# A two-layer FNet and gated-MLP kernel: layer 2's down products of blocks two to four in seven products for eight

## The chip, the cores and the metric

The kernel runs on one core of one Trainium2 chip. The time is the device time of one execution, in microseconds, and what counts is the median of several runs. TensorE (PE) multiplies matrices out of SBUF into PSUM banks; VectorE (DVE), ScalarE (ACT) and GpSimd (POOL) work on tiles; SyncE (SP) issues most of the DMA transfers. Each engine works through its own instructions in the order in which they stand.

## The reference, cut to what matters

```python
def layer(x):                      # x: 2048 x 640, fp32; run twice
    n = layernorm(x)
    a, b = n @ hid_re.T, n @ hid_im.T            # DFT along the hidden axis
    x = x + seq_re @ a - seq_im @ b              # DFT along the sequence, real part
    n = layernorm(x)
    h = sigmoid(n @ w_gate) * (n @ w_up)         # 640 -> 1728
    return x + h @ w_down                        # 1728 -> 640
```

The DFT matrices are inputs. The three weights are random with a spread of 0.4 (0.05 times 8). All is fp32.

## The kernel before, in words

**Numbers in two parts.** TensorE works on f16. Each operand is the sum of a high part (a cast, on ScalarE) and a low part (what the cast left, on VectorE), and each product takes three passes, high by high, high by low and low by high (`PASSES`). `split` (L266) makes the parts of a weight.

**Tokens and tiles.** The 2048 rows of x lie in SBUF as 16 tiles of 128, in four blocks of four (here called blocks 1 to 4; the code counts from 0). A block's four tiles are called GA, GB, GC and GD; for the DFT they hold even and odd rows of two halves of the sequence. The 1728 columns of the gated part are 13 tiles of 128 and half a tile.

**One layer.** First the DFT, folded by the symmetries of its matrices. Then each block in turn goes through gate and up, and then down. A step of gate and up does two of the 13 tiles, j and j+1, for the block's 512 tokens, and the half tile comes last. From layer 2's block 1 and layer 1's block 2 on, gate and up already run as seven products of 256 columns where the plain way has eight (`seven`; `part_one` to `part_seven` are its products, L1446, and what empties PSUM): sums of the quarters of x and of the weights are multiplied, and sums of the results are the four quarters wanted. What the previous pair of tiles still needs (the gate's sigmoid, the multiplication by up in `up`, and the cast and low part in `up_parts`, L1508 to L1514) is worked off within the next pair's step. `gate_tail` (L1585 to L1590) does the half tile.

**Down** is plain in both layers: for each of the block's four row tiles and each half of the 640 columns, 13 x 3 + 2 products of 320 columns (L1603), added into x by one VectorE instruction a half (L1618). A row tile of layer 2 is then stored by `store_x` (L438): GA and GD by SP's queue (L447), GB and GC by rows, from POOL's queue (L442), the very last from ACT's.

**The next block's x.** While a block is worked on, x of the next one is normalised and turned, in pairs of row tiles: `pair_apply` and `pair_combine` (L603 to L614) and `pair_parts` (L621, L622) on VectorE and ScalarE, then two transposing transfers on SP's queue (`pair_transpose`, L628). They are written into one of two buffers `XW`; `place` (L574) says which, by turns.

**Weights.** Their f16 parts and the sums for the seven products are made in layer 1 and kept in DRAM; `load_s` (L1362) brings a tile's parts back on SP's queue for each block. `test_w` (L262 in its cost: a largest absolute value) tests in layer 2 that the weights lie within bounds.

**Tests of symmetry.** The folding is right only if the DFT matrices have the symmetries, so the matrices are read beside the work, in pieces: a load on POOL's queue (L1664, L1681, L1724), a few operations of VectorE (`test_rows`, L1670 to L1673, and the like), and squares summed up on ScalarE (L1636). At the end a flag is read, and where it is set a general path computes all anew. Before, 51 of the 84 tests of the sequence's matrices are in layer 1, and the tests of the hidden ones are in layer 2, block 3 and later.

**What sets the order.** The program is a list of steps (14 slots of gate and up and 8 of down a block). A table of calls `at(u, f)` puts each job at a place u in units of steps, and the jobs of a step are written out ahead of its products, or at four places within a `seven` step. SBUF is one tile `big`, whose pieces get their addresses from a planner (`find_homes`) in a first pass.

```python
for j0, j1 in ((0, 7), (7, NF + 1)):
    steps.append(down(b, i, j0, j1, not first))
...
u = block[b] - 8 + 1.2 * i
...
at(u + 1.1, pair_transpose, b, i, not first and b == last)
```

## Time and profile before

| | us |
|---|---|
| median of three runs (lowest, highest) | 1135.03 (1135.00, 1135.28) |
| span of the profiled execution, first to last instruction | 1133.3 |
| TensorE busy | 1117.1 (99%) |
| VectorE busy | 757.7 (67%) |
| ScalarE busy | 539.9 (48%) |
| GpSimd busy | 346.8 (31%) |
| DMA, mean over the span | 189 GB/s |

The profiled execution's own time isn't among the three; its span leaves out what lies ahead of the first instruction and behind the last, 1.7 us against the median.

In the profile, "busy" counts an engine's working instructions. A row of a group reads: line of the code, engine, operation, destination <- source, count, busy time and mean time of one, and then the idle time ahead of them with what ended most of it. A row of waits reads: engine and what it stood for, what released it, and then the total, the count and the longest. A row of the chain of waits or of the timeline begins with the start in us and the duration. A window's row gives start and end, length, and then the busy time of PE, PEld, DVE, ACT, POOL with counts, the granted clock of TensorE, the busy share of the DMA engines and GB/s. Layer 2's blocks lie at these times of the trace: block 1 at 654 to 754 us, block 2's gate and up until 834 and its down until 878.5, block 3 until 958.4 and 1003, block 4 until 1083 and 1127.6.

### The profile page before, as it was taken

The page shows a single profiled execution, that of the slowest core. Times are in us where ns is not written, and L with a number is a line of the kernel's source. Part 1 is how long each engine was busy: PE and PEld are TensorE (multiplying, and loading weights), DVE is VectorE, ACT ScalarE, POOL GpSimd, SP SyncE. Part 2 cuts the span into 40 slices and gives each one's busy share as a digit, 9 for nine tenths or more (in the row PEclk, how much of TensorE's full clock was granted, in tenths as well). Part 3 has the DMA queues.
Part 4 walks back from the last instruction along what each step waited for, and adds up shares of the span by engine and source line. Part 5 has one row for each costly group of instructions (what it writes and reads, how often), then busy time and mean ns, then how long its engine had stood idle before and what let it go on. Part 6 is the DMA issues. An engine that isn't in the chain of part 4 may idle for free. (4 is left out here: it accounts for less than half of the span.)

```text
span 1133.3 us, 23690 instructions
## 1 busy us (share of the span) xinstructions
PE 1117.1 (99%) x9112; PEld 891.3 (79%) x9112; DVE 757.7 (67%) x1679; ACT 539.9 (48%) x1191; POOL 346.8 (31%) x568
## 2 busy tenths in 40 slices
PE   7999999999999999999999999999999999999997
PEld 5767446788878887788878888778877888788875
DVE  7984897856756776576667877834764678526751
ACT  7985583355525653256525545314542555225430
POOL 1001653343455354322340203031554222132001
PEclk9999999999999999999999999999999999999999
DMA  7633885878597756778521772585857873998411
GB/s 241 194 107 103 311 314 154 247 221 256 156 223 225 256 183 159 205 240 309 165 94 53 195 228 83 136 234 179 257 172 171 280 256 103 115 247 261 167 42 39
DMA packets 154448, 214.74 MB, mean 189 GB/s; under 512 B 74655, under 2 KB 99505, under 8 KB 154326
## 3 DMA queue, kind: packets, MB, share of 16 engines
q1 hardware_dynamic: 135622, 165.04, 50.0%
q0 software_dynamic: 18560, 47.93, 14.4%
q8 instruction: 73, 1.20, 0.4%
...
## 5 line engine op out<-in xcount | busy, mean ns | idle before, releaser
L1446 PE MATMUL acc<-big 128*128 128x256 f16 x4698 | 516.4, 273 | 0.0
L1446 PEld LDWEIGHTS <-big 128*128 128x128 f16 x4698 | 459.7, 98 | 54.3
L1603 PE MATMUL acc<-big 128*128 128x320 f16 x2624 | 357.7, 299 | 0.0
L1603 PEld LDWEIGHTS <-big 128*128 128x128 f16 x2624 | 256.8, 98 | 99.5
L1450 ACT ACTIVATE big<-acc 128x256 f32<-128x256 f32 x348 | 131.1, 382 | 261.8 <-PE acc L1446 259.4
L1664 POOL DMA_DIRECT2D big<-in_ct x256 | 174.3, 686 | 249.5 <-DVE big L1673 110.3
L1514 DVE TENSOR_TENSOR big<-big 128x512 f16<-128x512 f32 x87 | 59.9, 688 | 111.6 <-ACT big L1513 111.5
L1636 ACT ACTIVATE big<-big 128x768 f32<-128x768 f32 (+10 forms) x110 | 81.3, 739 | 83.9 <-DVE big L1673 56.6
L1399 PE MATMUL acc<-big 128*128 128x256 f16 (+1 forms) x705 | 114.7, 325 | 0.3 <-ACT big L678 0.3
L1399 PEld LDWEIGHTS <-big 128*128 128x128 f16 x705 | 68.9, 98 | 44.9 <-issue 0.6
L1618 DVE SCALAR_TENSOR_TENSOR big<-acc,big 128x320 f32<-128x320 f32 x64 | 28.4, 483 | 74.3 <-PE acc L1603 74.3
L1492 ACT ACTIVATE big<-big 128x512 f32<-128x512 f32 x87 | 53.2, 627 | 44.5 <-DVE big L1483 43.8
L271 DVE SCALAR_TENSOR_TENSOR big<-big 128x640 f16<-128x640 f32 (+7 forms) x82 | 61.4, 779 | 11.1 <-ACT big L269 8.8
L1502 DVE SCALAR_TENSOR_TENSOR big<-acc,big 128x256 f32<-128x256 f32 x87 | 36.4, 418 | 48.2 <-PE acc L1446 42.7
L269 ACT ACTIVATE big<-big 128x640 f16<-128x640 f32 (+7 forms) x82 | 51.3, 658 | 21.0 <-POOL big L1337 6.6
L1483 DVE TENSOR_TENSOR big<-big,acc 128x512 f32<-128x512 f32 x87 | 59.2, 680 | 2.9 <-PE acc L1446 2.6
L1513 ACT ACTIVATE big<-big 128x512 f16<-128x512 f32 x87 | 54.4, 625 | 7.6 <-DVE big L1504 6.5
L1681 POOL DMA_DIRECT2D big<-in_ct x40 | 27.3, 688 | 92.2 <-ACT big L1636 55.9
L621 ACT ACTIVATE big<-big 128x384 f16<-128x384 f32 (+2 forms) x48 | 28.6, 646 | 52.3 <-DVE big L603 34.5
L442 POOL DMA_INDIRECT out<-big,rows x8 | 9.5, 1187 | 133.4 <-DVE fin L1761 53.6
L1482 DVE TENSOR_TENSOR big<-big 128x256 f32<-128x256 f32 x87 | 36.3, 417 | 8.8 <-ACT big L1450 8.7
L622 DVE TENSOR_TENSOR big<-big 128x384 f16<-128x384 f32 (+2 forms) x48 | 34.2, 750 | 7.1 <-DMA big<-big 7.0
(252 smaller groups left out, 1089.2 us busy)
## 6 DMA issues: line engine op xcount, KB each, us to landing
...
big<-kept_w SPq DMA_DIRECT2D x115, 320.0 KB, 4.8
big<-in_ct POOLq DMA_DIRECT2D x256, 128.0 KB, 5.1
...
kept_w<-big SPq DMA_DIRECT2D x27, 320.0 KB, 3.7
...
big<-in_wg SPq DMA_DIRECT2D x18, 320.0 KB, 4.9
```

Of the source, the lines that this page charges most:

```text
L269: nc.scalar.activation(dh, src, AF.Copy, scale=s)
L271: nc.vector.scalar_tensor_tensor(dl, src, s, dh, op0=OP.mult, op1=OP.subtract)
L1399: nc.tensor.matmul(ps, w[wp][:, d * P : (d + 1) * P], xt[:, xp, :], start=(d == 0 and wp == HI and xp == HI), stop=(d == ND - 1 and wp == LO))
L1446: nc.tensor.matmul(ps, wt, xt, start=start and n == 0, stop=n == len(todo) - 1, skip_group_check=not start)
L1450: nc.scalar.activation(dst, ps, AF.Copy)
L1483: nc.vector.tensor_tensor(v, v, other, op=OP.add)
L1492: nc.scalar.activation(v, v, AF.Sigmoid, scale=SG)
L1513: nc.scalar.activation(s.parts[HI], v, AF.Copy)
L1514: nc.vector.tensor_tensor(s.parts[LO], v, s.parts[HI], op=OP.subtract)
L1603: nc.tensor.matmul(held["pd", e][0][:, :EH], held["ht", j].parts[hp][:, i * P : (i + 1) * P], held["w", 2, j].parts[wp][:, e * EH : (e + 1 ...
L1636: nc.scalar.activation(v, v, AF.Square, accum_out=new_sum()[:p])
L1664: nc.gpsimd.dma_start(v[:, g], bass.AP(ct.tensor, (r * S + row) * S, [[P, NS], [d * S, 16], [1, P]]))
```

## The change

**Down in seven products.** In layer 2's blocks 2 to 4 (`MADE`), twelve of the F tiles are taken as six pairs (`mates`). The pair is the inner dimension's two halves, the rows of the left side are {GA, GB} and {GC, GD}, and the columns are the two halves of 320. `mated_down` multiplies seven combinations (A11, A12, A22 and sums S1 to S4 of the left, three halves of the weights and four combinations of them on the right), for two row tiles each, into PSUM banks that are added into x at several points: 16 adds a block where there were 8. The 13th tile and the half tile stay plain. `mates_sums` makes the four sums of a pair on VectorE, `mates_parts` and `mates_rest` the casts and low parts of seven quarters where there were four. The result of `part_seven` is now added straight from PSUM by VectorE, where ScalarE copied it out first (not in a block's last step).

**Weights.** The four combinations of each of the six pairs of down weights are made in layer 1's blocks 2 and 3 (`load_mates`, `make_mates`, `split_mates`, `keep_mates`), in the buffer of x that is free then, kept in DRAM, and loaded once in layer 2's block 2 (`load_t`) into places that have come free: one of the two buffers `XW` among them. From then on `place` gives blocks 2 to 4 of layer 2 the one that is left.

**Places.** The pair work on the next block's x stands later, and so do its transposes and the first weight loads. Each test of symmetry has its own places for load, work and squares in `TESTS` and `HIDDEN` (46 in layer 1, 38 in layer 2); `test_w` of the down weights moves from layer 2's block 3 into layer 1's downs (`DOWNS`). The stores of GB and GC of blocks 2 and 3 come after the next block's start (`block + 1.3`). Within the made downs, jobs are written out in between the products (`due`). The bound on the weights' size goes from 16 to 4.

```diff
-WMAX = 16.0
+WMAX = 4.0
...
+NP = 6
+MADE = {(1, 1), (1, 2), (1, 3)}
+TESTS = [(0, 1, 5.5, 6.7, 7.2), (0, 1, 12.5, 14.2, 14.7), (0, 1, 18.0, 19.2, 19.7), (0, 1, 18.5, 19.7, 20.2), (0, 1, 19.0, 20.2, 20.7), (0, 1, 20.0, 21.2, 21.7),
...
+DOWNS = [(0, 18.6), (0, 19.1), (0, 19.6), (0, 20.1), (1, 19.1), (1, 19.6),
...
+MATES = [(5.7, 7.2, 7.5), (7.3, 8.7, 9.0), (8.8, 11.2, 11.5), (5.7, 7.2, 7.5), (7.3, 8.7, 9.0), (8.8, 11.2, 11.5)]
...
     def place(b):
-        return (b + len(other)) % 2
+        return 0 if other and b else (b + len(other)) % 2
...
+    def load_mates(m):
+        for j in (2 * m, 2 * m + 1):
+            nc.sync.dma_start(fixed(made_at(m) + 5 * (j % 2), 5, "tr", j).f32, wd[j * P : (j + 1) * P, :])
+
+    def make_mates(m):
+        a, b = (held["tr", j].f32 for j in (2 * m, 2 * m + 1))
+        v = fixed(made_at(m) + 10, 10, "tf", m).f32
+        t1, t2, t3, t4 = (v[:, EH * n : EH * (n + 1)] for n in range(4))
+        nc.vector.tensor_tensor(t1, a[:, EH:], a[:, :EH], op=OP.subtract)
+        nc.vector.tensor_tensor(t3, b[:, EH:], a[:, EH:], op=OP.subtract)
+        nc.vector.tensor_tensor(t2, b[:, EH:], t1, op=OP.subtract)
+        nc.vector.tensor_tensor(t4, b[:, :EH], t2, op=OP.subtract)
+        for j in (2 * m, 2 * m + 1):
+            drop("tr", j)
+
...
+    def load_t(m):
+        pin = (0, 10, XU + XTU, XU + XTU + 10, XU + XTU + 20, FIX)[m]
+        nc.sync.dma_start(take(10, "T", m, pin=pin).f16, kept["t", m])
+
...
-    def part_seven(b, j):
+    def part_seven(b, j, last):
         chain, _, _, _, _, w = held["step", j]
         products(chain, b, j, [("S3", "T3"), ("UM", "x1M")])
-        snap(w[:, :256], chain)
-
-    def part_three(b, j):
+        if last:
+            snap(w[:, :256], chain)
+        else:
+            nc.vector.tensor_tensor(w[:, :256], chain, w[:, 256:], op=OP.add)
+
+    def part_three(b, j, last):
         _, _, other, ko, v, w = held["step", j]
         products(other[:, 256:], b, j, [("S4", "x11"), ("GM", "x1M")])
-        nc.vector.tensor_tensor(w[:, :256], w[:, :256], w[:, 256:], op=OP.add)
-        nc.vector.tensor_tensor(v, v, other, op=OP.add)
+        if last:
+            nc.vector.tensor_tensor(w[:, :256], w[:, :256], w[:, 256:], op=OP.add)
+        both = other.rearrange("p (h c) -> p h c", h=2)
+        nc.vector.tensor_tensor(v[1], v[1], both, op=OP.add)
...
+        if ("hv", j) not in held:
+            if j % 2:
+                mates_parts(j - 1, "hA")
+                mates.append(j - 1)
...

...
             up(earlier[0])
+            mates_sums()
             some(1)
             part_four(b, earlier[1])
             for i in js:
                 part_five(b, i)
             up_parts(earlier[0])
             up(earlier[1])
+            if not last:
+                mates_rest()
             some(2)
             if last:
                 tail(ps, 1)
                 drop("w", 3, 0)
             for i in js:
-                part_seven(b, i)
+                part_seven(b, i, last)
+            if last:
+                mates_rest()
...
+    A11, A12, A22, S1, S2, S3, S4 = range(7)
+
+    def mated_down(b, store):
+
+        accs = {}
+        last = b == NB - 1
+
+        def left(m, q, hp, p):
+            name, o = (("hA", 0), ("hA", 1), ("hB", 0), ("hS", 0), ("hS", 1), ("hR", 0), ("hR", 1))[q]
+            return held[name, 2 * m].parts[hp][:, 256 * o + P * p : 256 * o + P * (p + 1)]
+
+        def right(m, w, wp):
+            if w < 3:
+                return held["w", 2, 2 * m + (w > 0)].parts[wp][:, EH * (w == 2) : EH * (w == 2) + EH]
+            return held["T", m].parts[wp][:, EH * (w - 3) : EH * (w - 2)]
+
+        def products_of(p, n, q, w, start, stop):
+            out = [(m, hp, wp) for m in range(NP) for hp, wps in PASSES for wp in wps]
+
+            def one(k, m, hp, wp):
+                if (p, n) not in accs:
+                    accs[p, n] = bank()
+                nc.tensor.matmul(accs[p, n][0][:, :EH], left(m, q, hp, p), right(m, w, wp), start=start and k == 0,
+                                 stop=stop and k == len(out) - 1, skip_group_check=True)
+
+            return [(one, k, *t) for k, t in enumerate(out)]
+
...
+        def add(p, n, g, e, free):
+            ps, k = accs[p, n]
+            xe = X[:, b * TB + g, e * EH : (e + 1) * EH]
+            nc.vector.scalar_tensor_tensor(xe, ps[:, :EH], CB, xe, op0=OP.mult, op1=OP.add)
+            if free:
+                del accs[p, n]
+                free_bank(k)
+
...
+        todo = []
+        for p in range(2):
+            todo += products_of(p, "a", A11, 0, True, True) + [(add, p, "a", p, 0, False)]
+        for p in range(2):
+            todo += products_of(p, "c", A12, 1, True, False)
+        todo += [(done, "hA")]
+        for p in range(2):
+            todo += products_of(p, "a", S2, 4, False, True) + [(add, p, "a", p, 1, False)]
+        for p in range(2):
+            todo += plain(p, "c", p, 0, False) + [(add, p, "c", p, 0, True)]
+        for p in range(2):
+            todo += products_of(p, "d", S1, 3, True, True) + [(add, p, "d", p + 2, 1, False)]
+        todo += [(done, "hS")]
+        for p in range(2):
+            todo += products_of(p, "a", S3, 5, False, True) + [(add, p, "a", p + 2, 1, False)]
+        for p in range(2):
+            todo += plain(p, "e", p + 2, 1, True) + [(add, p, "e", p + 2, 1, True)]
+        for p in range(2):
+            todo += products_of(p, "a", A22, 6, False, False) + plain(p, "a", p + 2, 0, False)
+            todo += [(add, p, "a", p + 2, 0, True)] + ([(put, p + 2)] if last or p else [])
+            todo += [(done, "hB")] if p else []
+            q = 1 - p
+            todo += products_of(q, "d", S4, 2, False, False) + plain(q, "d", q, 1, False)
+            todo += [(add, q, "d", q, 1, True)] + ([(put, q)] if last or p else [])
+        marks = [n for n, t in enumerate(todo) if t[0].__name__ == "one"]
+        cuts = [0] + [marks[len(marks) * k // 8] for k in range(1, 8)] + [len(todo)]
+
+        def step(k):
+
+            def mm(due):
+                for n in range(cuts[k], cuts[k + 1]):
+                    if n == 38:
+                        mates_rest()
+                    if (n - cuts[k]) % 6 == 0 and n > 38:
+                        due((n - cuts[k]) / (cuts[k + 1] - cuts[k]))
+                    f, *a = todo[n]
+                    f(*a)
+                due(1)
+
...
+            return mm, post, False
+
+        return [step(k) for k in range(8)]
 
...
-            for i in range(TB):
+            for i in range(TB) if (layer, b) not in MADE else ():
...
+            if (layer, b) in MADE:
+                steps += mated_down(b, not first)
...
-                u = block[b] - 8 + 1.2 * i
+                slow = (layer, b - 1) in MADE
+                u = block[b] - 6.9 + 1.8 * i if slow else block[b] - 8 + 1.2 * i
...
-                    at(u + 0.2 + 0.2 * n, pair_parts, b, i, n)
-                at(u + 1.1, pair_transpose, b, i, not first and b == last)
+                    at(u + (0.4 + 0.3 * n if slow else 0.2 + 0.2 * n), pair_parts, b, i, n)
+                at(u + (1.5 if slow else 1.1), pair_transpose, b, i, not first and b == last)
...
-                        at(u - 2 - 0.5 * (j % 2) if j > 3 else block[b] - ((5.9, 3, 2, 1.5) if first and b == 1 else (8, 7.9, 4.5, 3.5))[j], load_s, j, not first and b == last)
+                        at(u - 2 - 0.5 * (j % 2) if j > 3 else block[b] - ((5.9, 3, 2, 1.5) if first and b == 1 else (4.5, 4, 3, 2.2) if (layer, b - 1) in MADE else (8, 7.9, 4.5, 3.5))[j], load_s, j, not first and b == last)
...
-                at(block[2] + j - 0.3, test_w, 2, j)
+                at(block[DOWNS[j][0]] + DOWNS[j][1], test_w, 2, j)
...
+        for m in range(NP):
+            if first:
+                u, v, w = (block[1 + m // 3] + t for t in MATES[m])
+                at(u, load_mates, m)
+                at(v, make_mates, m)
+                at(w, split_mates, m, (0,))
+                at(w + 0.5, split_mates, m, (1,))
+                at(w + 1.0, keep_mates, m)
+            else:
+                at(block[1] + 1 + m, load_t, m)
...
+                for g in (GB, GC) if made else ():
+                    at(block[b + 1] + 1.3, store_x, b, g, slice(0, D))
...
+        for (load, test, key), (l, b, u, v, w) in zip(tests, TESTS):
+            if l == layer:
+                at(block[b] + u, load, *key)
+                at(block[b] + v, test, *key)
+                at(block[b] + w, square_rest)
...
+        def due(part):
+            while todo and todo[0][0] - u <= part:
+                _, f, a = todo.pop(0)
+                f(*a)
```

How this moves instructions is shown at two places. The first is VectorE at the entry into layer 2's block 2's down, where the gate and up's last work stands in front of the adds. Before:

```order
L1587 SCALAR_TENSOR_TENSOR big<-acc_65,big 64x512
L1590 TENSOR_TENSOR big<-big 64x512
L1670 TENSOR_TENSOR big<-big 128x256
L1671 TENSOR_TENSOR big<-big 128x256
L1673 TENSOR_TENSOR big<-big 128x128 x2
L1482 TENSOR_TENSOR big<-big 128x256
L1483 TENSOR_TENSOR big<-big,acc_483 128x512
L1502 SCALAR_TENSOR_TENSOR big<-acc_64,big 128x256
L1504 SCALAR_TENSOR_TENSOR big<-big 128x256
L1514 TENSOR_TENSOR big<-big 128x512
```

After, the same stretch and what follows it (L1726 and L1729 are the half tile, L1577 and L1579 are `part_three`, L1628 to L1631 the four sums, L1599 and L1601 `up`, L1616 `up_parts`, L1807 the adds into x, L1640 the low parts of a pair):

```order
L1726 SCALAR_TENSOR_TENSOR big<-acc_65,big 64x512
L1729 TENSOR_TENSOR big<-big 64x512
L1577 TENSOR_TENSOR big<-big 128x256
L1579 TENSOR_TENSOR big<-big,acc_483 128x512
L1628 TENSOR_TENSOR big<-big 128x256
L1629 TENSOR_TENSOR big<-big 128x256
L1630 TENSOR_TENSOR big<-big 128x256
L1631 TENSOR_TENSOR big<-big 128x256
L1599 SCALAR_TENSOR_TENSOR big<-acc_64,big 128x256
L1601 SCALAR_TENSOR_TENSOR big<-big 128x256
L1616 TENSOR_TENSOR big<-big 128x512
L1807 SCALAR_TENSOR_TENSOR big<-acc_480,big 128x320
```

The test of rows (L1670 to L1673) has gone from here, four sums have come between `part_three` and `up`, and the first add into x stands right behind the last tile's low part.

The second is SP's queue ahead of layer 2's block 4, with the two transposing transfers of each pair of row tiles. Before:

```order
L1363 DMA big_63<-kept_w_0_0_1146 128x1280
L1365 DMA big_63<-kept_s_0_2103 128x2048
L1367 DMA big_63<-kept_w_1_0_1163 128x1280
L1363 DMA big_63<-kept_w_0_1_1182 128x1280
L1365 DMA big_63<-kept_s_1_2204 128x2048
L1367 DMA big_63<-kept_w_1_1_1199 128x1280
L628 DMA_TRANSPOSE big_63<-big_63 128x17x128 x2
L447 DMA out_0<-big_63 128x640
L628 DMA_TRANSPOSE big_63<-big_63 128x17x128 x2
L1363 DMA big_63<-kept_w_0_2_1253 128x1280
```

After (L679 are the transposes, L1447 to L1451 the loads of a tile's gate parts, sums and up parts):

```order
L679 DMA_TRANSPOSE big_63<-big_63 128x17x128 x2
L1447 DMA big_63<-kept_w_0_0_1146 128x1280
L1449 DMA big_63<-kept_s_0_2103 128x2048
L1451 DMA big_63<-kept_w_1_0_1163 128x1280
L1447 DMA big_63<-kept_w_0_1_1182 128x1280
L1449 DMA big_63<-kept_s_1_2205 128x2048
L1451 DMA big_63<-kept_w_1_1_1199 128x1280
L679 DMA_TRANSPOSE big_63<-big_63 128x17x128 x2
L1447 DMA big_63<-kept_w_0_2_1253 128x1280
```

The first pair's transposes now stand ahead of the loads of tiles 0 and 1, and the second pair's behind them; the store of a row tile between them is elsewhere.

233 lines of the change are left out of this document (160 added, 73 removed), and 13 rows, old and new, of the table TESTS.

## The prediction

> **What bounds the kernel now.** I read the page first, then what TensorE (PE) waited for, then the chain of waits.
>
> ```profile
> PE 1117.1 (99%) x9112; PEld 891.3 (79%) x9112; DVE 757.7 (67%) x1679; ACT 539.9 (48%) x1191; POOL 346.8 (31%) x568
> PEclk9999999999999999999999999999999999999999
> L1603 PE MATMUL acc<-big 128*128 128x320 f16 x2624 | 357.7, 299 | 0.0
> ```
> ```profile
> PE twin L404 <- DMA big<-in_x: 6.1, 3, 3.9
> ...
> PE acc L1036 <- DVE big L900: 0.8, 1, 0.8
> ```
> ```profile
> 709.51 44.55 PE acc L1603 x328
> ...
> 833.98 44.55 PE acc L1603 x328
> 878.53 71.40 PE acc L1446 x654
> ...
> 1083.02 44.57 PE acc L1603 x328
> ...
> 1127.62 0.49 DVE big L1618
> ```
>
> PE is busy 99% of the span at a granted clock of 0.9 or more in every slice. What it waits for lies at the start (twin, the turning of x) or between the layers (L1036, 0.8 us at most at once). From 709.5 us to the end the chain of waits is PE alone, one product behind the other. So in layer 2 each product removed shortens the program by its own spacing, as long as nothing else comes late. A down of one block is 328 products in 44.55 us, 0.1358 us each (the 299 ns of the group is one product's latency, not its spacing). A gate-and-up product of 256 columns takes 71.40 / 654 = 0.1092 us.
>
> **The change, part by part.**
>
> *Fewer products.* A block's down was 4 x 2 x (13 x 3 + 2) = 328 products. Now 12 of the 14 rows of tiles go in six pairs: 7 combinations x 2 x 6 pairs x 3 passes = 252, and the last two rows take 8 x (3 + 2) = 40. That is 292, so 36 fewer in each of three blocks: 108 x 0.1358 = **-14.67 us**, all on the path. The shape (128x320) stays.
>
> *VectorE (DVE) and ScalarE (ACT) in the gate-and-up steps.* For two rows of tiles, VectorE gets four sums of 256 columns, and the low parts are taken of 1,792 columns instead of 1,024.
>
> ```profile
> L1514 DVE TENSOR_TENSOR big<-big 128x512 f16<-128x512 f32 x87 | 59.9, 688 | 111.6 <-ACT big L1513 111.5
> L1482 DVE TENSOR_TENSOR big<-big 128x256 f32<-128x256 f32 x87 | 36.3, 417 | 8.8 <-ACT big L1450 8.7
> L1450 ACT ACTIVATE big<-acc 128x256 f32<-128x256 f32 x348 | 131.1, 382 | 261.8 <-PE acc L1446 259.4 <-DMA big<-kept_w 0.3 <-DVE big L1482 0.3
> ```
> ```profile
> 878.50:958.40 79.90, 79.90 (x734) 71.60 (x732) 57.82 (x134) 43.04 (x99) 22.34 (x42) 1.00 0.67 219
> ```
> ```profile
> L262 DVE TENSOR_REDUCE wmax<-big 128x1 f32<-128x640 f16 x14 | 11.3, 804 | 0.0
> ```
>
> That is 4 x 0.417 + 0.688 + 0.417 = 2.77 us more a pair, 16.6 us in six. The fullest window of layer 2 is block 3's gate-and-up (the third block; the kernel counts from 0 and calls it block 2): VectorE 57.8 of 79.9 us. There the change takes away the 14 weight tests (11.3 us, now in layer 1's downs) and adds eight tests of the hidden matrix, at most 8 x 0.69 us by the nearest row (512 columns). So 57.8 + 16.6 - 11.3 + 5.5 = 68.6 of 79.9 us, 86%: under PE's time. ScalarE loses two copies out of PSUM a pair (2 x 0.382) and gets three more casts' worth of 768 columns, about 1 us: no change. The add of part seven now reads PSUM on VectorE; the next product into that bank comes 30 products into the next step, behind 18 of part three, so it has (18 + 30) x 0.1092 = 5.2 us. I cost all this at nothing. The cover is PE's own 11.8 us a pair (108 x 0.1092). Without it the price is what VectorE needs above 11.8 us, 18 times; see the rivals.
>
> *The entry into a down.* Here a queue is long. The products start with A11 (36) and A12 (36); then S2 goes into A11's bank, so the two adds that read it must be done 72 x 0.1358 = 9.8 us after the entry, and the last pair's S parts soon after. Before, at block 2's entry (833.98):
>
> ```profile
> 833.71 0.69 DVE L1587 SCALAR_TENSOR_TENSOR big<-acc,big 64x512 f32<-64x512 f32 x1
> 835.09 0.69 DVE L1590 TENSOR_TENSOR big<-big 64x512 f16<-64x512 f32 x1 [0.69 <-ACT big L1588]
> 835.81 0.43 DVE L1670 TENSOR_TENSOR big<-big 128x256 f32<-128x256 f32 x1
> ...
> 837.02 0.42 DVE L1482 TENSOR_TENSOR big<-big 128x256 f32<-128x256 f32 x1
> ...
> 838.91 0.42 DVE L1502 SCALAR_TENSOR_TENSOR big<-acc,big 128x256 f32<-128x256 f32 x1 [0.76 <-ACT big L1492]
> ...
> 840.42 0.69 DVE L1514 TENSOR_TENSOR big<-big 128x512 f16<-128x512 f32 x1 [0.76 <-ACT big L1513]
> ```
> ```profile
> 832.33 0.62 ACT L1513 ACTIVATE big<-big 128x512 f16<-128x512 f32 x1
> 832.98 0.59 ACT L1586 ACTIVATE big<-acc 64x512 f32<-64x512 f32 x1
> ```
>
> ScalarE gets three casts ahead of these two (0.65 + 0.65 + 0.3, the spacing of its rows), so L1587 moves to 835.3 and L1590 to 836.7. The test of rows behind it (835.81 to 837.02, 1.2 us) is gone, so L1482 comes at 837.4 instead of 837.02. The four sums then take 4 x 0.34 = 1.35 us while ScalarE makes the gate; the multiplies come at 839.8 instead of 838.91, the last low part at 841.3 instead of 840.42, and the two adds are done at 842.9. PE needs them at 843.8. The margin is 0.9 us, and for the first hA part (needed 15 products in, 836.0; cast at 834.6) 1.4 us. I take 0 us of stall. If the queue is 2 us longer than this it is 1.1 us a block, 3.3 us; a gain is excluded, PE being full there.
>
> *One buffer for the transposed x instead of two.* The transposes of the next block must wait for this block's last gate-and-up product, and they stand 5.4 and 3.6 steps ahead of the next block (a step is 4.96 us now) with the loads of two weight tiles between them on SP's queue.
>
> ```profile
> 845.34 6.18 SPq L628 DMA_TRANSPOSE big<-big  x2
> ...
> 859.78 6.43 SPq L628 DMA_TRANSPOSE big<-big  x2
> ```
> ```profile
> 970.04 12.39 SPq L628 DMA_TRANSPOSE big<-big  x2
> ...
> 984.12 13.74 SPq L628 DMA_TRANSPOSE big<-big  x2
> ```
> ```profile
> DMA to landing us min/median/max: 8.3/9.4/11.1
> ```
> ```profile
> 853.12 1.14 DVE L603 TENSOR_SCALAR big<-big,small 128x640 f32<-128x640 f32 x2 [5.50 <-DMA big<-big]
> ...
> 855.89 2.63 DVE L622 TENSOR_TENSOR big<-big 128x384 f16<-128x384 f32 x4
> ```
>
> VectorE finishes the entry 10.3 us into the down (842.9 and three low parts, 1.4 us), each of two tile pairs takes 5.4 us (853.12 to 858.5), and about six adds stand between them, 0.4 us each: the second is ready at 23.5 us. Its second transpose is issued half of 6.2 us later and lands 9.4 us after that: 36 us, and the block needs it at 292 x 0.1358 = 39.7 us. With the slow issue of 970 to 998 us (13.74) it is 23.5 + 6.9 + 11.1 = 41.5: 1.8 us late. That was beside small-packet loads of the hidden matrix, which the change puts elsewhere; three test loads now lie there for block 3, none for block 4. So 0 to 1.8 us at each of two blocks; I take 0.5 us in all, near the quiet rows. The Trainium skill speaks against this: "DMA: Bandwidth & Descriptors", Queues, rings and completion order, says that each DMA engine takes turns packet by packet between the queues that have work, so that the tests' loads on another queue would take their share from the transposes. The doubled issue at 970 us (12.39 against 6.18) agrees; by the rule alone block 3's start would be the 1.8 us late.
>
> *Layer 1.* Six pairs of weights are combined on VectorE in blocks 2 and 3 (24 operations of 320 columns, six casts and differences of 1,280), with 12 loads, 6 stores of 640 KB. A long operation:
>
> ```profile
> 642.51 1.35 DVE L651 TENSOR_TENSOR big<-big 128x1152 f16<-128x1152 f32 x1
> ```
> ```profile
> 475.00:555.00 80.00, 80.00 (x732) 71.36 (x730) 52.68 (x120) 45.31 (x102) 19.95 (x34) 1.00 0.73 244
> ```
>
> By it a mate costs 1.5 us for the difference and 4 x 0.48 (L1618's row of 320 columns, below) for the combinations: 3.4 us, 10 us a block of 80, in place of tests that move out. The tests go to block 4: 19 in its gate-and-up window (475 to 555) instead of about ten, nine more x 0.5 MB, 56 GB/s on 244. At 0.73 busy now, that is about 0.9. I take nothing; if the weight loads come late there, up to 3 us. The four operations of a row test are 1.2 us (835.81 to 837.02), 11 us more on VectorE's 52.7 of 80: no bound.
>
> *The end.*
>
> ```profile
> L1618 DVE SCALAR_TENSOR_TENSOR big<-acc,big 128x320 f32<-128x320 f32 x64 | 28.4, 483 | 74.3 <-PE acc L1603 74.3
> ```
> ```profile
> out<-big SPq DMA_DIRECT2D x6, 320.0 KB, 2.6
> ```
> ```profile
> 1128.14 0.38 ACTq L447 DMA_DIRECT2D out<-big  x1
> ```
>
> The last store was half a row of tiles (160 KB, issued at 1128.14, the span ends at 1133.3); now it is a whole one of 320 KB. At the 300 GB/s or so that 320 KB in under 2.6 us and the windows bear out, the second half is 0.5 us: **+0.5 us** (0 to 1.3, half of 2.6). The 16 adds instead of 8 a block (0.483 us) lie beside 40 us of PE.
>
> *Sum.* -14.67 + 0 + 0.5 + 0.5 = -13.7 us. The profiled execution's span is 1133.3 us; the median of the three times is 1135.03, so 1.7 us lie around the span, unchanged. **1135.0 - 13.7 = 1121.3 us.**
>
> **The rivals.**
>
> *Late at the seams (0.20).* The entry queue and the transposes are both late by their worse ends: 3.3 + 2 x 1.8 + 3 in layer 1 is at most 9.9, a typical half of it 5 us: 1126. For it: the margin at the entry is 0.9 us, out of a sum of ten terms. Against it: in the before trace PE never waited there, though VectorE was queued for 7 us past the same entry.
>
> *VectorE paces the pairs, slower (0.05).* VectorE works in order, and each low part waits for a cast of ScalarE (L1514's 111.5 us in 68 waits, 1.6 us each). A pair now has four such waits. Its work is 68.6 / 79.9 x 11.8 = 10.1 us; with one wait uncovered 11.7, with two 13.3 us. From 12.6 us on (13.7 / 18 = 0.8 us over PE's 11.8) the gain is gone; at 13.3 us it is 18 x 1.5 - 13.7 = 13 us slower: 1148. Against it: the order of VectorE's work puts the sums and the other tile's multiplies between a cast and its use, and PE's deadlines for a bank lie 5 to 8 us behind.
>
> *The products don't go (0.01).* If the symmetry or size tests failed, the general path would run after all and the time would be a multiple. The new bound of 4 on the weights is ten times their spread of 0.4, so I leave it.
>
> **How the numbers follow.** The forecast case has 0.74: 1120.4 (nothing late, no longer end) to 1123.5. The range reaches into the seams' case: 1120.0 to 1126.5. About 0.2% (2.3 us) is what a measurement here can tell from no change. Faster: the forecast, nearly all of the seams and a part of VectorE's case, 0.94; within 0.2%: 0.02; slower: 0.04.
>
> **What would show it.** Each of the last three downs should be 292 products in 39.7 us, block 1's still 44.55. PE's waits should name no VectorE add (S2's start) over 0.5 us and no transposing DMA at a block's start. VectorE should be below 90% in the gate-and-up of blocks 2 to 4. The forecast is wrong if a pair takes over 11.9 us on PE there, or if PE's idle time between 710 us and the end sums to over 3 us.

## The result, and the profile after

| | before | after |
|---|---|---|
| median, us | 1135.03 | 1155.24 |
| lowest to highest (4 runs each) | 1135.00 to 1135.28 | 1149.11 to 1157.52 |
| ratio to before (95% interval) | | 1.0166 (1.0137 to 1.0195) |
| span of the profiled execution | 1133.3 | 1155.0 |

The change is slower, by 1.7%, and its executions now differ among themselves by 8 us. The 108 products are gone as forecast. (One of b1's five executions below took 1658.8 us at a granted clock of 0.66; its ratio leaves that one out.) The page of after:

```profile
PE 1110.4 (96%) x9004; PEld 883.2 (76%) x9004; DVE 829.5 (72%) x1841; ACT 530.8 (46%) x1153; POOL 345.4 (30%) x568
PEclk9999999999999999999999999998999998999999
```

TensorE has 9004 products where it had 9112, and is busy 96% where it was 99%: it now waits. Its waits over the whole span, and the chain, name what for:

```profile
PE acc L1530 <- DMA big<-kept_w: 20.2, 5, 10.4
```
```profile
769.04 15.21 DMA big<-kept_w
784.25 0.02 issue
784.27 22.60 DMA big<-kept_w
...
909.88 9.05 DMA big<-kept_w
...
954.29 21.63 DMA big<-in_wh
...
988.40 14.67 PE acc L1787 x108
```

Two loads of gate weights in block 2 take 15.2 and 22.6 us from issue to landing; in this stretch before, such loads landed in 2.9 us (median). In block 3 the chain also goes through a load of the hidden matrix (`in_wh`), which takes 21.6 us. The windows of layer 2, cut at the blocks. Before, block 2's gate and up, its down, and block 3's gate and up; after, the same three, then block 3's down and block 4's gate and up:

```profile
753.90:833.82 79.92, 79.92 (x735) 71.62 (x733) 44.22 (x115) 40.86 (x95) 30.11 (x53) 1.00 0.63 201
833.82:878.37 44.55, 44.55 (x331) 32.09 (x328) 23.94 (x56) 12.50 (x24) 17.08 (x24) 1.00 0.71 173
878.37:958.28 79.91, 79.91 (x735) 71.62 (x733) 57.83 (x135) 43.04 (x99) 22.47 (x42) 1.00 0.67 218
```
```profile
758.05:854.19 96.14, 82.17 (x735) 72.07 (x733) 59.54 (x156) 42.45 (x101) 47.39 (x77) 0.95 0.81 233
854.19:893.85 39.66, 39.66 (x294) 28.57 (x292) 28.73 (x64) 11.50 (x21) 5.61 (x8) 1.00 0.67 174
893.85:988.24 94.39, 85.24 (x734) 73.90 (x732) 61.85 (x148) 45.59 (x111) 36.81 (x50) 0.95 0.74 200
988.24:1027.91 39.67, 39.67 (x295) 28.57 (x293) 25.25 (x52) 9.74 (x17) 0.24 (x2) 1.00 0.64 161
1027.91:1108.17 80.26, 80.21 (x734) 71.59 (x732) 60.68 (x125) 35.78 (x99) 2.14 (x2) 1.00 0.52 182
```

Each made down takes 39.66 us, all of them TensorE at work, and the next block's gate and up starts without a wait. The loss is in the gate and up of block 2 (96.14 for 79.92) and block 3 (94.39 for 79.91). By these rows TensorE stands for 14.0 and 9.2 us of them, and takes 2.3 and 5.3 us longer for the same products, at a granted clock of 0.95 in the mean. With block 1's down beginning at 713.50 for 709.35, the span's change adds up: +4.15 up to there, +16.2 and +14.5 in the two stretches, +0.2 in block 4's, 3 x -4.9 = -14.7 in the downs, and +1.3 at the end make +21.7.

What the DMA engines had to do in the first 49 us of block 2's gate and up, before and after (count, KB each, median time to landing):

```profile
DMA packets 4762, 9.66 MB, mean 197 GB/s; under 512 B 570, under 2 KB 2333, under 8 KB 4756
...
big<-kept_w SPq DMA_DIRECT2D x9, 320.0 KB, 2.9
big<-in_ct POOLq DMA_DIRECT2D x13, 128.0 KB, 6.9
```
```profile
DMA  0176799899999999999999999999999999999999
...
DMA packets 4841, 12.76 MB, mean 260 GB/s; under 512 B 908, under 2 KB 1818, under 8 KB 4836
...
big<-in_ct POOLq DMA_DIRECT2D x41, 128.0 KB, 8.2
big<-kept_t SPq DMA_DIRECT2D x6, 640.0 KB
...
big<-kept_w SPq DMA_DIRECT2D x5, 320.0 KB
```

The engines are full in nearly every slice. 41 pieces of tests (13 before) and the six sets of combinations are issued, and five tiles of gate weights where there were nine.

Full engines alone are not enough to make TensorE wait. Before, they were nearly as full in the first half of blocks 3 and 4, and TensorE worked all the time:

```profile
878.50:921.00 42.50, 42.50 (x392) 38.09 (x390) 26.82 (x62) 22.64 (x54) 10.57 (x16) 1.00 0.89 290
...
1003.00:1044.00 41.00, 41.00 (x377) 36.69 (x376) 20.74 (x40) 18.69 (x47) 11.09 (x11) 1.00 0.98 281
```

In that stretch of block 4 the tests asked for ten loads of 200 KB beside the weights, 2 MB. In block 2 of after, tests and combinations ask for 41 x 128 KB and 6 x 640 KB, about 9 MB in 49 us.

### The profile page after: what moved, and what is told of

Same layout as the page of the kernel before. It is cut to its first block, busy times and chain, and to the rows that moved or that the text cites. A ratio compares the mean times of both kernels' runs of the same rounds, so it can differ in the third digit from the quotient of the medians.

```text
span 1155.0 us, 23700 instructions
## 1 busy us (share of the span) xinstructions
PE 1110.4 (96%) x9004; PEld 883.2 (76%) x9004; DVE 829.5 (72%) x1841; ACT 530.8 (46%) x1153; POOL 345.4 (30%) x568
## 3 DMA queue, kind: packets, MB, share of 16 engines
q1 hardware_dynamic: 138934, 176.67, 51.2%
## 5 line engine op out<-in xcount | busy, mean ns | idle before, releaser
L1530 PE MATMUL acc<-big 128*128 128x256 f16 x4698 | 524.1, 274 | 26.4 <-DMA big<-kept_w 20.2
L1530 PEld LDWEIGHTS <-big 128*128 128x128 f16 x4698 | 461.8, 98 | 86.0 <-DMA big<-kept_w 21.4
L1742 PE MATMUL acc<-big 128*128 128x320 f16 x1640 | 223.6, 299 | 0.0
L1742 PEld LDWEIGHTS <-big 128*128 128x128 f16 x1640 | 160.5, 98 | 62.2
L1534 ACT ACTIVATE big<-acc 128x256 f32<-128x256 f32 x268 | 99.0, 380 | 212.2 <-PE acc L1530 204.9
L1787 PE MATMUL acc<-big 128*128 128x320 f16 x756 | 105.6, 299 | 0.0
L1483 PEld LDWEIGHTS <-big 128*128 128x128 f16 x705 | 68.9, 98 | 44.9 <-issue 0.6
L1787 PEld LDWEIGHTS <-big 128*128 128x128 f16 x756 | 74.0, 98 | 28.6
L322 DVE SCALAR_TENSOR_TENSOR big<-big 128x640 f16<-128x640 f32 (+8 forms) x88 | 71.1, 835 | 9.2 <-ACT big L320 6.9
L320 ACT ACTIVATE big<-big 128x640 f16<-128x640 f32 (+8 forms) x88 | 58.9, 699 | 35.3 <-DMA kept_t<-big 9.4
L1599 DVE SCALAR_TENSOR_TENSOR big<-acc,big 128x256 f32<-128x256 f32 x87 | 36.4, 418 | 49.1 <-PE acc L1530 41.8
L1616 DVE TENSOR_TENSOR big<-big 128x512 f16<-128x512 f32 x51 | 35.0, 687 | 47.2 <-ACT big L1615 46.9
L1579 DVE TENSOR_TENSOR big<-big,acc 128x512 f32<-128x512 f32 x87 | 56.1, 680 | 1.3 <-PE acc L1530 1.1
L1807 DVE SCALAR_TENSOR_TENSOR big<-acc,big 128x320 f32<-128x320 f32 x48 | 23.0, 488 | 41.8 <-PE acc L1798 29.5
L1640 DVE TENSOR_TENSOR big<-big 128x512 f16<-128x512 f32 x72 | 41.5, 618 | 13.7 <-ACT big L1639 13.2
L1919 DVE TENSOR_TENSOR big<-big 128x256 f32<-128x256 f32 x64 | 26.7, 417 | 22.2 <-DMA big<-in_ct 22.2
```

The source lines that it names most:

```text
L320: nc.scalar.activation(dh, src, AF.Copy, scale=s)
L322: nc.vector.scalar_tensor_tensor(dl, src, s, dh, op0=OP.mult, op1=OP.subtract)
L1483: nc.tensor.matmul(ps, w[wp][:, d * P : (d + 1) * P], xt[:, xp, :], start=(d == 0 and wp == HI and xp == HI), stop=(d == ND - 1 and wp == LO))
L1530: nc.tensor.matmul(ps, wt, xt, start=start and n == 0, stop=n == len(todo) - 1, skip_group_check=not start)
L1534: nc.scalar.activation(dst, ps, AF.Copy)
L1579: nc.vector.tensor_tensor(v[1], v[1], both, op=OP.add)
```

## The experiments

Theory A was that too much is put on the DMA engines at once; B that the combinations' loads hold up SP's queue; C that the new VectorE and ScalarE work paces the steps. From the second group on, D is that the tests' loads come late and VectorE, working in order, stands for them; A2 is A in a cruder form, that a block's bytes are too many wherever they stand. Times are medians; the stretches in the table are from each run's profiled execution, a single one. Where a stretch has the same work in several runs, these differ: block 2 is 96.1, 95.8 and 93.5 us in after, e3 and e4, and block 3 is 94.4, 97.1 and 91.2 in after, e2 and e4. Smaller differences than these, in stretches with waits, say nothing.

| run | time, us | start of block 1's down, against before | gate and up 2, 3, 4 | downs 2, 3 |
|---|---|---|---|---|
| before | 1135.0 | 0 | 79.9, 79.9, 80.0 | 44.55, 44.55 |
| after | 1155.2 | +4.2 | 96.1, 94.4, 80.3 | 39.66, 39.67 |
| e1, no tests in gate and up 2, 3 | 1138.3 | +6.0 | 87.5, 80.9, 82.0 | 39.66, 39.67 |
| e2, combinations late | 1150.0 | +4.7 | 90.6, 97.1, 79.9 | 39.67, 39.67 |
| e3, no hidden tests in block 3 | 1146.7 | +4.0 | 95.8, 83.3, 80.3 | 39.67, 39.66 |
| e5, places without the made downs | 1159.3 | +9.7 | 87.4, 87.3, 79.9 | 44.55, 44.56 |
| e6, no tests | 1125.3 | +2.0 | 79.9, 79.9, 82.0 | 39.66, 39.66 |
| e8, early places | 1168.4 | +16.6 | 80.1, 79.9, 89.0 | 47.9, 51.5 |
| e9, same, casts later | 1157.4 | +4.5 | 80.1, 79.9, 90.2 | 47.0, 51.2 |
| e10, longer lead | 1158.8 | +16.3 | 97.5, 88.9, 80.3 | 39.66, 39.66 |
| e4, casts later | 1153.1 | +0.1 | 93.5, 91.2, 80.3 | 39.67, 39.66 |
| b1, even places | 1126.5 | +0.2 | 79.9, 80.9, 84.6 | 40.6, 39.66 |
| b2, same, space early | 1126.3 | +0.9 | 79.9, 80.6, 84.4 | 39.8, 39.66 |
| b4, columns last | 1127.8 | +2.5 | 79.9, 79.9, 82.9 | 39.7, 39.66 |
| b5, same, combinations early | 1132.6 | +3.4 | 83.4, 79.9, 81.4 | 39.67, 39.66 |
| b6, all repaired | 1131.1 | +0.2 | 80.2, 79.9, 85.8 | 40.2, 39.66 |
| b7, columns between | 1129.8 | +0.8 | 79.9, 79.9, 85.9 | 39.66, 39.66 |

**Which part costs.** e1:

```diff
-            if l == layer:
+            if l == layer and not (l == 1 and (b == 2 or b == 1 and u < 15)):
...
+                if b == 2:
+                    continue
```


> Leaves out the tests of symmetry whose loads lie in gate and up of layer 2's blocks 2 and 3 (12 of the sequence's matrices in block 2, 10 in block 3, 8 of the hidden ones in block 3); all else as in the changed kernel. There, these two gate-and-up stretches took 96.1 and 94.4 us where the kernel before has 79.9. Theory A (the DMA engines have more to move there than they can: weights, combinations and tests together): both stretches fall to 80 to 82 us and the time to 1123 to 1128 us. Rival B (the loads of the combinations hold up the weight loads behind them on SP's queue): block 2 stays over 90 us, block 3 falls to 80, 1138 to 1143 us. Rival C (VectorE and ScalarE, with the sums and low parts, pace the steps): both shorten by no more than the tests' own VectorE work, 3 us each, and stay over 90 us.

Measured 1138.3 us (it is 13 tests in block 2, not 12): block 2 is 8.7 us shorter and block 3 13.5. Block 3 comes to 80.9 as A says, so VectorE's sums do not pace it (C). Block 2 stays at 87.5, between A's 82 and B's 90 (and the time is in B's range), with one wait of 5.05 us at its start: in block 1's down two tests were left. Their place shows in the profile of after, too:

```profile
752.19 0.43 DVE L1919 TENSOR_TENSOR big<-big 128x256 f32<-128x256 f32 x1 [10.71 <-DMA big<-in_ct]
```

VectorE stands 10.7 us there for a test's load (7.0 in e1), with the adds of the down behind it. That gave theory D.

e2 and e3:

```diff
-                at(block[1] + 1 + m, load_t, m)
+                at(block[1] + 7 + m, load_t, m)
```


> Loads the six sets of combinations six steps later in layer 2's block 2 (steps 7 to 12, not 1 to 6); all tests stay. Theory A: the tests and weights alone fit better in the first half, and the second half, with 0.65 of the DMA engines busy, takes the 3.9 MB: the stretch falls from 96.1 to 82 to 88 us, the time to 1143 to 1149. Rival B: the hold-up moves with the loads and the stretch stays within 3 us of 96. Rival C: no change, since no engine's work changes.

1150.0 us; block 2 at 90.6. A third of its loss went. The rest stayed, with a wait of 3.0 us for ScalarE early and one of 4.5 us for weights in the second half: between A and B, and against C.

```diff
             for (load, test, key, n), (l, b, u, v, w) in zip(tests, HIDDEN):
+                if b == 2:
+                    continue
```


> Leaves out the eight tests of the hidden matrices in layer 2's block 3 (their loads are small packets); all else as in the changed kernel. Theory A: block 3's gate and up falls from 94.4 to 82 to 86 us (one wait of 2.7 us for weights lies ahead of the hidden tests and stays), the time by 8 to 12 us, block 2 keeps its 96. Rivals B and C: block 3 keeps over 90 us, as eight short VectorE operations (5 us) are all that goes.

1146.7 us, block 3 at 83.3, block 2 unchanged (95.8): as A says. The hidden tests are 11 of block 3's 14.5 us.

e5 takes the made downs out and leaves the places:

```diff
-MADE = {(1, 1), (1, 2), (1, 3)}
+MADE = set()
...
-        return 0 if other and b else (b + len(other)) % 2
+        return (b + len(other)) % 2
...
-                at(block[1] + 1 + m, load_t, m)
+                pass
...
-            at(block[1] - 8, slots.now)
-            at(block[1] - 8, slots.hole, XU + XTU, XTU)
```


> The downs of layer 2's blocks 2 to 4 are plain again (328 products, 44.55 us each), with two buffers for the turned x and the earlier places of its transposes, and without the loads of the combinations; the places of the tests, layer 1's work on the combinations and the add of part seven stay as changed. Theory A: block 2's gate and up, with 3.9 MB less, takes 80 to 84 us, block 3's, with the hidden tests, still 88 to 94; layer 1 stays 3.6 us longer: 1147 to 1154 us. Rival B: block 2 and block 3 both at 80 us, 1139 us. Rival C: the same 1139 us, since the sums and low parts are gone.

1159.3 us: with no sums, no combinations to load and plain downs, the places alone make the kernel 24 us slower than before. B and C fall as the main cause. A's numbers were missed too: block 2 takes 87.4 us where A had 80 to 84, and 9.7 us are lost ahead of block 1's down where it had 3.6. Why is open, since the planner also gave other addresses here.

e6 takes away all tests:

```diff
-            if l == layer:
+            if l == 2:
...
-            for (load, test, key, n), (l, b, u, v, w) in zip(tests, HIDDEN):
+            for (load, test, key, n), (l, b, u, v, w) in ():
```


> Leaves out all 84 tests of the sequence's matrices and the 14 of the hidden ones; all else as in the changed kernel, the combinations' loads and the made downs included. Theory D (the tests' new places are at fault: their loads come late, VectorE and ScalarE, which take their work in order, stand for them, and TensorE follows): all that is lost against the forecast comes back, layer 1 within 2.5 us of before (the wait for the store of the combinations stays), every gate and up of layer 2 at 80 to 81 us: 1120 to 1125 us. Rival A2 (too many bytes whatever they are for): block 2, with 3.9 MB of combinations in its first half, stays over 84 us: 1126 to 1130. Rival C (the sums and low parts pace the steps): made blocks' gate and up over 84 us each, 1134 us or more.

1125.3 us (0.9913, 0.9896 to 0.9929). The made blocks with all their sums, low parts and 3.9 MB of combinations:

```profile
755.89:835.80 79.91, 79.91 (x735) 71.62 (x733) 43.09 (x101) 31.11 (x73) 5.67 (x16) 1.00 0.53 177
835.80:875.46 39.66, 39.66 (x295) 28.57 (x292) 25.25 (x52) 9.63 (x17) 0.00 (x0) 1.00 0.66 159
875.46:955.37 79.91, 79.91 (x735) 71.62 (x732) 42.77 (x100) 31.12 (x73) 7.69 (x18) 1.00 0.44 142
```

TensorE is busy in every us of them. So the loss is that of the tests beside the rest; what the downs bring is there. Block 4 is 2 us long, which the expectation didn't have, for another reason: ScalarE stands there for a row store (a store of GB or GC from GpSimd's queue) whose space it is given,

```profile
1010.78 0.66 ACT L1534 ACTIVATE big<-acc 128x256 f32<-128x256 f32 x2 [9.27 <-DMA out<-big,rows]
```

because the stores of GB and GC now come behind the block's start, and the planner hands the space on 0.1 step later.

**Where the tests stand.** e8 gives the tests the places of before (by its formula) and has e2's edit; e9 adds the casts of e4:

```diff
-TESTS = [(0, 1, 5.5, 6.7, 7.2), (0, 1, 12.5, 14.2, 14.7), (0, 1, 18.0, 19.2, 19.7), (0, 1, 18.5, 19.7, 20.2), (0, 1, 19.0, 20.2, 20.7), (0, 1, 20.0, 21.2, 21.7),
+TESTS = [(0, 0, 28.0, 29.457, 30.368), (0, 0, 29.167, 30.624, 31.535),
...
+HIDDEN = [(1, 2, 15.5, 18.7, 19.18), (1, 2, 17.45, 20.65, 21.13),
```


> All tests are kept, but at the places that the kernel before gives them (51 in layer 1, 33 in layer 2, the hidden ones from block 3's down on), and the combinations are loaded in steps 7 to 12 of layer 2's block 2; made downs, sums and the work on the combinations as changed. Theory D: the waits of VectorE for tests go back to those of before; block 1 of layer 2 at 56.3 us again, block 2 and 3 at 80 to 82; the transposes into the one buffer may come late beside the hidden tests (up to 4 us at block 4): 1121 to 1129 us. Rival A2: block 2 with 12 tests and the combinations stays over 88 us: 1132 us or more. Rival C: over 1134.

1168.4 us, a miss. Blocks 2 and 3 do come to 80.1 and 79.9, with 12 tests and the combinations in block 2, which speaks against A2. But block 2's down takes 47.9 us, as TensorE waits 1.3 and 3.8 us for VectorE's adds, which have tests among them. Block 3's down takes 51.5, up to block 4's first product, and block 4's gate and up 89.0. The hidden tests now run beside the transposes into the one buffer:

```profile
1008.90 20.77 SPq L664 DMA_TRANSPOSE big<-big  x2
```
```profile
1029.98 0.37 PE L1515 MATMUL acc<-big 128*128 128x256 f16 x1 [11.24 <-DMA big<-big]
```

The pair of transposes is issued in 20.8 us (9.7 in after), and TensorE waits 11.2 us for them at the block's start. This is the prediction's seam, six times dearer than its worse end, where the change had taken the hidden tests out of its way. By the Trainium skill ("DMA: Bandwidth & Descriptors", Queues, rings and completion order) each DMA engine takes turns between the queues that have work; the 20.8 us agree with that, and so does after, where hardly a test stood beside the transposes and no block's start was late.

> As the run with the earlier places, and in layer 1 the second and third pair of combinations are cast one step later in each of two blocks, so that the store of the pair ahead has landed when ScalarE comes to the cast. If ScalarE's wait for that store (4.7 us, twice) is what costs layer 1's blocks 2 and 3 about 1 us each, these come to 79.9 us and the time falls by 1.5 to 2.5 us against the run with the earlier places; if it is VectorE's 1.4 us operations on the combinations, nothing changes.

1157.4 us, 11 less than e8, all ahead of layer 2's block 1's down. Layer 1's block 2 comes from 86.8 to 79.9 us, its block 3 from 89.6 only to 84.4, with a wait of 2.6 us for weights. So the store costs, as the run expected, but here several times the size: ScalarE's waits for it were 8.2 and 9.9 us in e8. In after it shows so:

```profile
279.54 1.27 ACT L320 ACTIVATE big<-big 128x1280 f16<-128x1280 f32 x1 [4.75 <-DMA kept_t<-big]
```

ScalarE comes to the cast of the second pair when the first pair's store still reads the buffer, and everything behind it waits. e4 alters that alone in the changed kernel:

```diff
-MATES = [(5.7, 7.2, 7.5), (7.3, 8.7, 9.0), (8.8, 11.2, 11.5), (5.7, 7.2, 7.5), (7.3, 8.7, 9.0), (8.8, 11.2, 11.5)]
+MATES = [(5.7, 7.2, 7.5), (7.3, 8.7, 10.0), (8.8, 11.2, 12.5), (5.7, 7.2, 7.5), (7.3, 8.7, 10.0), (8.8, 11.2, 12.5)]
```


> The changed kernel with one thing altered: in layer 1, the casts of the second and third pair of combinations in each of blocks 2 and 3 come one step later. By the store that ScalarE waits for, blocks 2 and 3 of layer 1 come from 81.1 to 79.9 us each in gate and up, and the rest stays: 1147 to 1156 us, the changed kernel's spread less 2. If VectorE's long operations on the combinations are the cause, both stay at 81.

1153.1 us, and block 1's down of layer 2 begins 0.1 us after before's, for 4.2. Blocks 2 and 3 of layer 1 are at 79.9 each, for 81.1 and 81.0, as they are in all b runs, which have this edit too: 2.3 of the 4.2 us are this store. Another 1.5 us were lost in layer 1's block 4, where ScalarE stood 4.3 us for another store (`kept_o`), and TensorE 0.9 for ScalarE and 0.2 for weights. In e4 that block takes 79.9, but in b4, with the same places in layer 1, it is 2.7 us long, by three waits for weights. So it varies from execution to execution, and e4 doesn't show that it hung on the casts.

e10 gives the tests more time:

```diff
-         (0, 1, 20.5, 21.7, 22.2), (0, 2, 0.0, 1.2, 1.7),
+         (0, 1, 20.5, 22.2, 22.7), (0, 2, 0.0, 1.7, 2.2),
```


> The changed kernel with all tests' loads where they are, and their VectorE work and squares half a step (2.9 us) later. Theory D: VectorE's waits for the tests' loads (22.2 and 19.7 us in all in the changed kernel) fall by half, and the time by 4 to 10 us, to 1145 to 1152. Rival A2 and C: within the spread of the changed kernel, 1149 to 1158, as neither bytes nor work change.

1158.8 us, no better. In the profiled execution, the slowest of five (1165.4 us), 16.3 us are lost ahead of block 1's down for 4.2 in after, which the expectation didn't have; why is open. Its waits of VectorE for the row tests, and of TensorE:

```profile
DVE big L1904 <- DMA big<-in_ct: 6.3, 2, 6.1
...
DVE big L1905 <- DMA big<-in_ct: 5.1, 5, 1.8
```
```profile
PE acc L1515 <- DMA big<-kept_w: 12.2, 7, 3.4
```

VectorE's waits fell from 41.9 us (22.2 and 19.7) to 11.4, and block 2 still takes 97.5 us: four of TensorE's five waits there, 9.1 of 11.8 us, are for weights. D falls as the main cause of block 2. It has a part in block 3: there e10's waits (6.7 us) are for ScalarE and VectorE, and in after one of 2.3 us, at 977, is for VectorE, behind the late load of the hidden matrix.

**Repairing it.** b1 keeps all tests and the made downs; it has e2's and e4's edits, and new tables, of which the first entries of blocks 2 and 3, of the hidden rows and of the hidden columns are:

```diff
+         (1, 1, 0.6, 2.16, 3.0), (1, 1, 1.55, 3.11, 3.95),
...
+         (1, 2, 0.3, 1.86, 2.7), (1, 2, 1.25, 2.81, 3.65),
...
+HIDDEN = [(1, 3, 2.5, 4.9, 5.4), (1, 3, 3.75, 6.15, 6.65),
...
+         (1, 3, -0.5, 1.9, 2.4), (1, 3, 1.0, 3.4, 3.9), (1, 3, 12.4, 14.8, 15.3), (1, 3, 12.8, 15.2, 15.7),
...
-                at(block[b + 1] + (1.4 if made else 0.9), slots.hole, 20 * b, 20)
+                at(block[b + 1] + (2.5 if made else 0.9), slots.hole, 20 * b, 20)
```


> All tests kept, made downs as changed. Layer 2's tests spread evenly: ten in block 1's gate and up, none in its down, 14 each in blocks 2 and 3 at 0.95 step apart with more time to their work (1.56 and 2.4 steps for 1.2 and 1.7), the hidden ones in block 4 at 1.25 steps apart; the combinations loaded in steps 7 to 12 of block 2; in layer 1 the casts of the second and third pair one step later; the space of a stored block of x given out at 2.5 steps for 1.4. Theory A (too much at once for the DMA engines, by where the tests and loads stand): block 2 and 3 at 80 to 81 us, downs at 39.7, block 4 at 80 to 82, layer 1 1 to 2 us longer than before: 1122 to 1127 us, below the kernel before. If it is the sum of bytes of a block and not where they stand, block 2 stays over 86 us: 1131 us or more.

1126.5 us, 0.9915 (0.9900 to 0.9931) of before: faster than both kernels, with the same work as after. Block 2's gate and up has 14 tests (13 in after) and the same combinations and takes 79.9. Block 4 is 4.6 us long.

b2 is b1 without the last edit (1.4 again).

> As the run with even places, but the space of a stored block of x is given out at 1.4 steps into the next block as in the changed kernel. If ScalarE's waits for the row stores (9.3 us in the run without tests, 1.9 us of TensorE at block 4) come from tiles placed there, blocks 3 and 4 together are 1 to 3 us longer than in the run with even places; if they come from the stores' own lateness on GpSimd's queue, the two runs are the same.

1126.3 us, and block 4 as in b1. In both it is VectorE that waits, 7.2 us in b1 and 7.0 in b2, for a small table that GpSimd writes behind its two row stores (b1's row):

```profile
1010.88 0.21 DVE L1971 STREAM_TRANSPOSE big<-big 128x32 f32<-128x32 f32 x1 [7.21 <-POOL big L1970]
```

TensorE then waits 2.8 and 2.6 us for ScalarE, which waits for VectorE. ScalarE never comes to the space early here, so the run doesn't tell the two explanations apart.

b4 is b2 with the hidden columns last, the hidden rows from 2.0 on, 1.2 apart, and the tests of blocks 2 and 3 from 0.2 on, 0.9 apart; b5 is b4 with the combinations in steps 1 to 6:

```diff
-         (1, 1, 0.6, 2.16, 3.0), (1, 1, 1.55, 3.11, 3.95),
+         (1, 1, 0.2, 1.76, 2.6), (1, 1, 1.1, 2.66, 3.5),
...
-HIDDEN = [(1, 3, 2.5, 4.9, 5.4), (1, 3, 3.75, 6.15, 6.65),
+HIDDEN = [(1, 3, 2.0, 4.4, 4.9), (1, 3, 3.2, 5.6, 6.1),
...
-         (1, 3, -0.5, 1.9, 2.4), (1, 3, 1.0, 3.4, 3.9), (1, 3, 12.4, 14.8, 15.3), (1, 3, 12.8, 15.2, 15.7),
+         (1, 3, 10.9, 13.3, 13.8), (1, 3, 11.4, 13.8, 14.3), (1, 3, 11.9, 14.3, 14.8), (1, 3, 12.4, 14.8, 15.3),
```

> As the run with even places (space given out at 1.4 steps), but in block 4 the six tests of the hidden matrix's columns stand last (steps 10.9 to 13.4), so that VectorE no longer waits 7.2 us at the block's start for the table that GpSimd writes behind its two row stores; and the tests of blocks 2 and 3 end ahead of the downs (0.9 step apart from 0.2 on). If that wait is what block 4's 4.6 us come from, block 4's gate and up is at 80 to 81 us, block 2's down at 39.7, and the time 1120 to 1123 us. If it is the load of the DMA engines by the hidden tests, block 4 stays at 83 us or more and the time at 1125.

1127.8 us. Block 4 is 82.9: my expectation missed, since ScalarE now stands 10.1 us for the row store instead. Blocks 2 and 3:

```profile
756.35:836.26 79.91, 79.91 (x734) 71.62 (x732) 58.05 (x155) 42.50 (x99) 39.87 (x68) 1.00 0.88 259
...
875.96:955.87 79.91, 79.91 (x735) 71.62 (x732) 60.57 (x155) 42.07 (x99) 26.49 (x46) 1.00 0.62 205
```

28 tests and the combinations pass under 2 x 79.91 us of TensorE at work, with the DMA engines at 0.88 in block 2.

> As the run with the columns last, but the combinations are loaded in steps 1 to 6 of block 2, as in the changed kernel. Theory A in its narrow form (14 tests and 3.9 MB in one stretch fit when the tests are spread): block 2 takes 80 to 83 us, the time within 3 us of the run with the columns last. If the place of these loads ahead of the weights on SP's queue is what delays the weights, block 2 comes to 88 us or more and the time to 1129 or more.

1132.6 us, block 2 at 83.4. The early place of the combinations costs block 2 3.5 us with evenly spread tests; with none beside them (e6) it costs nothing. The block is just over A's 83, the time in B's range. TensorE's two waits (1.4 us for VectorE, 1.8 for weights) lie in the half that has the combinations, where the DMA engines are fuller (b5, then b4, first 48.7 us):

```profile
757.34:806.00 48.66, 46.17 (x422) 40.92 (x419) 28.67 (x75) 21.88 (x52) 18.60 (x28) 1.00 0.95 285
```
```profile
756.35:805.00 48.65, 48.65 (x448) 43.60 (x446) 30.34 (x79) 23.91 (x56) 19.57 (x29) 1.00 0.82 241
```

b6 is b4 with the space given out at 2.5 steps, layer 1's block 4 evened (0.83 apart) and the hidden tests earlier; b7 is b6 with the columns between the rows (the first line is b4's, the second b6's, the last pair b6's and b7's columns):

```diff
-HIDDEN = [(1, 3, 2.0, 4.4, 4.9), (1, 3, 3.2, 5.6, 6.1),
+HIDDEN = [(1, 3, 1.5, 3.9, 4.4), (1, 3, 2.6, 5.0, 5.5),
...
-         (1, 3, 9.7, 11.7, 12.2), (1, 3, 10.1, 12.1, 12.6), (1, 3, 10.5, 12.5, 13.0), (1, 3, 10.9, 12.9, 13.4),
+         (1, 3, 3.1, 5.5, 6.0), (1, 3, 4.7, 7.1, 7.6), (1, 3, 6.3, 8.7, 9.2), (1, 3, 7.9, 10.3, 10.8),
```

> As the run with the columns last, and the space of a stored block of x is given out at 2.5 steps for 1.4; layer 1's block 4 has its 27 tests at an even 0.83 step; the hidden tests of block 4 are done before its down. If the space handed out before the row store has landed is what makes ScalarE stand 10 us at block 4's start, block 4's gate and up comes from 82.9 to 80 to 80.5 us; layer 1's block 4 at 80 to 81 us; all downs of the made blocks at 39.7: 1121.5 to 1124.5 us. If block 4's loss is the hidden tests' load on the DMA engines, it stays at 82 us or more: 1125 us or more.

1131.1 us, a miss. ScalarE's 10 us at block 4's start are gone, as they should be if the space was their cause; the block is 85.8 all the same, by a new wait of 4.8 us at its end, where column tests stood close together in the queues of VectorE and ScalarE.

> As the run with all repaired, but the six column tests of block 4 stand between the eight row tests at 1.6 steps apart, not in two steps at the end, where VectorE and ScalarE took turns on four of them while ScalarE's copy out of PSUM stood behind and TensorE waited 4.8 us. If that packing is the cause, block 4's gate and up comes from 85.8 to 80 to 81 us and the time to 1121.5 to 1125 us. If the hidden tests' load on the DMA engines were at fault, TensorE would wait for weights and block 4 stay over 83 us.

1129.8 us, a miss: block 4 at 85.9, now by a wait for weights.

```profile
1055.82 15.60 PE L1515 MATMUL acc<-big 128*128 128x256 f16 x126 [3.55 <-DMA big<-kept_w]
```

Here the other branch of the expectation holds: with the hidden rows 1.1 steps apart from 1.5 on, the DMA engines are 0.96 busy from 994 to 1056 us and the weights come late at its end. In the six runs with the hidden tests at block 4 it is 1.4 to 5.9 us longer than before: by VectorE's wait for the table (b1, b2), ScalarE's for the row store (b4, b5), the column tests (b6) and weights (b7). A place for them that costs nothing was not found beside the made downs; before, with two buffers and ten of their loads in its first 41 us, block 4 took 80.0.

## Why the prediction was wrong, point by point

The prediction's own sign of being wrong came: it had set 3 us of TensorE's idle time from 710 us on, and there were 23.1 in two stretches.

- **Fewer products**: right. 39.66 us a down in every run with quiet surroundings, 4.89 us less, 14.7 in all (14.67 forecast).
- **VectorE in the steps**: right. Block 3 has 61.9 us of VectorE where 68.6 was forecast. In gate and up TensorE never waits for it directly without the tests (e6), and with them spread 1.4 us at most at once (b5). Of the rivals on the slower side, "VectorE paces the pairs" isn't what happened, and "The products don't go" isn't either; none was about loads.
- **The entry**: right to a tenth. The two adds were done at 863.2 us (862.35 and 0.88), 9.0 us after the entry at 854.19; they were needed at 9.8.
- **One buffer, transposes**: right in after (no wait at a block's start), with the hidden tests where they now stand; e8, with them beside the transposes, shows the seam at 11.2 us.
- **Layer 1**, "I take nothing; if the weight loads come late there, up to 3 us": wrong. It cost 4.2 us up to layer 2's block 1's down. 2.3 of them are ScalarE's waits for the store of the pair ahead (e4); I had counted 12 loads and 6 stores, and not asked what the next cast of the same buffer waits for. 1.5 are block 4's, where the weights that I feared were 0.2 us of TensorE's waiting in after, though all of it in b4 (2.2 us, the block 2.7 longer).
- **Layer 2's tests and combinations**: this is the step that failed. Of the eight hidden tests I priced the VectorE work ("at most 8 x 0.69 us") and not their loads; of the loads of six sets of 640 KB there is no term at all; and the tests' new places in blocks 2 and 3 were looked at only for VectorE and beside the transposes. "So 57.8 + 16.6 - 11.3 + 5.5 = 68.6 of 79.9 us ... I cost all this at nothing" named TensorE as the cover, but a load is covered only while the DMA engines bring it, and the weights beside it, in time. It cost 30.7 us: 16.2 in block 2 and 14.5 in block 3. That these are the loads' places, and not the sums or the low parts, e6 and b4 show: without tests, and with all tests spread, both stretches take 79.91 us. Whether the engines' own time is what ran out, or the order in the queues, the runs settle only in part (e2 and b5 lie between A and B). The rows to ask were there: block 3's gate and up had the DMA engines at 0.89 in its first half, and the hidden tests' loads doubled an issue of the transposes.
- **The end**: +1.3 us where 0.5 was taken; the upper bound was 1.3. The row of 320 KB in 2.6 us gives 126 GB/s, not the 300 that the 0.5 rests on, and half of 2.6 us was the better price.
- With places for the loads the sum very nearly holds: b2 has 1126.3 us, of which 4.3 are block 4's; the forecast was 1121.3. That is a subtraction (4.3 from the profiled execution); no run showed the number itself.
